# One block transformer decode step: 128 rows of the last gate's weights moved from the end of SP's queue to its beginning

## The chip, the core and the metric

One NeuronCore of a Trainium2 chip runs the whole program. The metric is the device time of one execution in microseconds (us); less is better. Three runs of the kernel before took 243.23, 243.19 and 242.94 us, median 243.19. PE is TensorE, DVE is VectorE, ACT is ScalarE, POOL is GpSimd, SP is SyncE, which here only issues DMAs. A DMA copies from the chip's memory (HBM) into SBUF, the cores' working memory of 128 partitions; sixteen DMA engines share the rows of each copy. PSUM holds the results of PE.

## What is computed

A decode step of one transformer block for four tokens (B = 4, D = 512). Six modulation vectors come from a condition `c`; attention over the last 2,048 entries of a cache, then a gated feed-forward part.

```python
mod = (_silu(c) @ w_mod).reshape(c.shape[0], 6, 1, -1)
sa, ca, ga, sb, cb, gb = (mod[:, 0], mod[:, 1], mod[:, 2], mod[:, 3], mod[:, 4], mod[:, 5])
h = _layernorm(x, axis=-1) * (1 + ca) + sa
x = x + ga * _A_ref(h, A_k_cache, A_v_cache, A_wq, A_wo)
h = _layernorm(x, axis=-1) * (1 + cb) + sb
x = x + gb * _B_ref(h, B_w1, B_w3, B_w2)
```

`_A_ref` is attention with 32 query heads over 8 key and value heads, head size 128, between the projections `wq` and `wo`. `_B_ref` is `(silu(x @ w1) * (x @ w3)) @ w2` with 1,792 hidden columns. All is float32. Some 101 MB are read once, most of it K and V. The last gate `gb` is `silu(c)` (4 x 512) times the last 512 columns of `w_mod` (512 x 512).

## The kernel before

Every weight and every piece of the cache comes by one long queue of DMAs that SP issues in a fixed, hand-written order (lines 91 to 125); ACT issues two more at the start, `t1_in` (the first query weights) and `x_in` (x, four rows). The order is: `t0_in` (c and the weights of sa and ca, into the first columns of the buffer KV1), the first K and V into KV0, the second K and V into KV1, then for each of four pairs of heads the weights WP and the next two K and V; at the end `wm_in` (weights of ga, sb, cb), `f1_in` and `f2_in` (w1 and w3), `gb_in` (the weights of gb) and six pieces of `w2_in`. Before an issue SP waits where its target is still in use: for `pe` 1 (KV1 still holds `t0_in`), `qt_done` (WP still holds query weights that are in use), `x_done` (a K and V has been used), `a_done`.

Each K and V is 128 rows of 64 KB, so KV0 and KV1 hold 8 MB each. The rows of a load are its partitions.

PE works through `main`, then four times through `pair` (scores, softmax turned on PE, values, output projection, for two heads) and `query` (the projection of the next queries), then `leave` and `post`. Other engines follow by semaphores that PE's instructions raise: `pe` counts the finished single steps. In `main` PE multiplies `sc`, the silu of c, by the weights of sa and ca into bank bM (8 products, line 255 by the helper `mm`), `pe` 1; then it transposes h (line 309), `pe` 2; then come the first queries.

The gate gb is made near the end: after `hid` has been put on its way, PE waits for `gb_in` (semaphore `dgb`), multiplies `sc` by its four blocks of 128 rows into four groups of partitions of bM, ACT copies the bank to `gb_sb` (line 458), and a product with `same` adds the four groups and turns the result (bT), which ACT copies to `gbJ`. Meanwhile PE takes w2 piece by piece as its six DMAs land. Behind the last piece DVE multiplies by gbJ (line 488), adds x1 (line 490), and SP stores the result (line 492).

```python
T.wait_ge(dgb, 16)
for k in range(4):
    ins = mm(bM[32 * k : 32 * k + B, :], sc[:, k * B : (k + 1) * B], KV[1][:, 6144 + 512 * k : 6144 + 512 * (k + 1)])
ins.then_inc(pe, 1)
A.wait((pe, 10))
t_gb = A.op(s.copy(gb_sb, bM))
```

Of the kernel before, what the change touches and what calls it, by code (L numbers as in the profile page):

```python
# [5 lines left out]
AF = mybir.ActivationFunctionType  # L6
# [4 lines left out]
B, D, HQ, G, SK, DH, W, FF = 4, 512, 32, 8, 8192, 128, 2048, 1792  # L11
P = 128
# [3 lines left out]
CHUNKS = [(j, c) for c in range(4) for j in range(4) if c < 2 or j < 3]  # L16
HEAD = 8
W2_CUTS = [0, 4, 8, 10, 12, 13, 14]
PAIRS = G // 2
# [23 lines left out]

def block_kernel(nc, x_in, t0_in, t1_in, kv_in, w_in, wm_in, f1_in, f2_in, gb_in, w2_in, out):
# [12 lines left out]
    A = Queue(nc, s, "act")  # L57
    V = Queue(nc, v, "dve")
    L = Queue(nc, gp, "pool")
    dx, dt0, dt1, dkv, dk, dva, dvb, dwo, dm, df1, df2a, df2b, dgb = sems("dx dt0 dt1 dkv dk dva dvb dwo dm df1 df2a df2b dgb")  # L60
    dw = sems(" ".join(f"dw{i}" for i in range(len(W2_CUTS) - 1)))
# [4 lines left out]
    KV = [sb("KV0", 16384), sb("KV1", 16384)]  # L66
    WP = sb("WP", 8192)
    T0 = KV[1][:, : 16 + 4096]
    x_sb = sb("x_sb", 512, B)
    ident, same, eps = sb("ident", P), sb("same", B), sb("eps", 1)  # L70
    sc, e1, e2 = sb("sc", 16), sb("e1", 16), sb("e2", 16)
    hT, h2T = sb("hT", 16), sb("h2T", 16)
    Z = sb("Z", B * 28)
    q_sb, p_sb, o_sb, a_sb, y_sb, g_sb, u_sb, gb_sb = [sb(n, 512) for n in "q_sb p_sb o_sb a_sb y_sb g_sb u_sb gb_sb".split()]
    pT = sb("pT", NT * B * 16)
# [12 lines left out]
    def load(dst, src, sem):  # L88
        S.dma_start(dst, src).then_inc(sem, 16)  # L89

    load(T0, t0_in, dt0)
    s.dma_start(WP[:, 4096:], t1_in).then_inc(dt1, 16)
    s.dma_start(x_sb, x_in).then_inc(dx, 16)
    load(KV[0], kv_in[0], dkv)
    S.wait_ge(pe, 1)
    load(KV[1], kv_in[1], dk)
    for p in range(PAIRS):
# [24 lines left out]
    load(KV[1][:, 3072:6144], f2_in[:, 3072:], df2b)  # L122
    load(KV[1][:, 6144:8192], gb_in, dgb)
    for a, b, sem in zip(W2_CUTS[:-1], W2_CUTS[1:], dw):
# [15 lines left out]
    for p in range(PAIRS - 1):  # L140
        gp.wait_ge(dk, 16 * (p + 1))
        for sem in (k_ok, va_ok, vb_ok):
            gp.sem_inc(sem, 1)
    for d, sem, n in ((dk, k_ok, 16 * PAIRS), (dva, va_ok, 16), (dvb, vb_ok, 16)):
        gp.wait_ge(d, n)
        gp.sem_inc(sem, 1)
# [24 lines left out]
    s.preload_act_table_set("natural_log_exp_and_others")  # L171
    for b_ in (bS, bQ, bO, bM):
        v_z = V.op(v.memset(b_, 0.0))
# [7 lines left out]
    A.wait((dt0, 16))  # L181
    t = A.op(s.activation(e1, T0[:, :16], AF.Exp, scale=-1.0))
    V.wait(t)
# [3 lines left out]
    V.wait(t, (dt0, 16))  # L187
    t_sc = V.op(v.tensor_mul(sc, T0[:, :16], e2))  # L188
# [7 lines left out]
    V.wait((pe, 2))  # L196
    t_hT = V.op(v.tensor_copy(hT, bT[:, :16]))  # L197
# [56 lines left out]
    def mm(o, lhsT, rhs, start=True, stop=True):  # L254
        return T.matmul(o, lhsT, rhs, start=start, stop=stop, skip_group_check=True)  # L255
# [47 lines left out]
    for k in range(4):  # L303
        for i in range(2):
            ins = mm(bM[32 * i : 32 * i + B, :], sc[:, k * B : (k + 1) * B], T0[:, 16 + (2 * k + i) * 512 : 16 + (2 * k + i + 1) * 512], k == 0, k == 3)
    ins.then_inc(pe, 1)
# [78 lines left out]
    ins.then_inc(pe, 1)  # L385
    A.wait((pe, 4))
    t_ga, t_sb, t_cb = [A.op(s.copy(dst, bX[32 * i : 32 * i + B, :])) for i, dst in enumerate((ga_sb, sb_sb, cb_sb))]

    V.wait((pe, 3), t_ga)
    t = V.op(v.tensor_mul(ag, bM[:B, :], ga_sb))  # L390
# [15 lines left out]
    ins.then_inc(pe, 1)  # L406
    V.wait((pe, 5))
    t_h2T = V.op(v.tensor_copy(h2T, bT[:, :16]))  # L408
# [11 lines left out]
    ins.then_inc(pe, 1)  # L420
    A.wait((pe, 6))
    t_g = A.op(s.copy(g_sb, bQ))
# [9 lines left out]
    ins.then_inc(pe, 1)  # L432
    A.wait((pe, 7))
    t = A.op(s.activation(view(eT), view(bP)[:, :, :, :B], AF.Exp, scale=-1.0))
# [7 lines left out]
    V.op(v.tensor_mul(view(hidT)[:, 0:2, 3], view(sT)[:, 0:2, 3], view(bP)[:, 2:4, 3, :B]))  # L442
    V.wait((pe, 8))
    t_u = V.op(v.tensor_copy(u_sb[:96], bA[:96]))
# [3 lines left out]
    ins.then_inc(pe, 1)  # L448
    V.wait((pe, 9))
# [12 lines left out]
    for i in range(len(W2_CUTS) - 1):  # L462
        T.wait_ge(dw[i], 16)
        for n in range(W2_CUTS[i], W2_CUTS[i + 1]):
            jj, c = CHUNKS[n]
            if n < HEAD:
                ins = mm(bO[32 * (n % 4) : 32 * (n % 4) + B, :], hw[:, c, jj, :], w2[:, n, :], n < 4, n >= HEAD - 4)
                continue
            for j in range(4):
                ins = mm(bX[32 * j : 32 * j + B, :P], hw[:, c, jj, :], w2[:, n, j * P : (j + 1) * P], n == HEAD, n == 13)  # L470
        if i == 0:
            T.wait_ge(A.sem, t_gb[1])
# [3 lines left out]
            A.wait((pe, 11))  # L476
            t_gb = A.op(s.copy(gbJ, bT[:, :P]))
        if i == 1:
            ins.then_inc(pe, 1)
            V.wait((pe, 12))  # L480
# [6 lines left out]
    V.wait((pe, 13), t_gb)  # L487
    t = V.op(v.tensor_mul(yt, bX[:, :P], gbJ))  # L488
# [8 lines left out]
def _layout(i):  # L497
    import numpy as np

    def a(t):  # L500
        return np.ascontiguousarray(t)

    k = i["A_k_cache"][:, :, SK - W :, :].reshape(B, G, NT, 512, DH)
    v = i["A_v_cache"][:, :, SK - W :, :].reshape(B, G, NT, 4, P, DH)
    k = k.transpose(1, 4, 2, 0, 3).reshape(G, P, 8192)
    v = v.transpose(1, 4, 2, 0, 3, 5).reshape(G, P, 8192)
    wm = i["w_mod"].reshape(4, P, 6, 512).transpose(1, 0, 2, 3)
    c = i["c"].reshape(B, 4, P).transpose(2, 1, 0).reshape(P, 16)
    wq = i["A_wq"].reshape(4, P, G, 512).transpose(2, 1, 0, 3).reshape(G, P, 2048)
# [5 lines left out]
    return {  # L515
        "x_in": a(i["A_x"].reshape(B, D)),
        "t0_in": np.concatenate([c, wm[:, :, 1::-1].reshape(P, 4096)], 1),
        "t1_in": np.concatenate([wq[0], wq[1]], 1),
        "kv_in": np.concatenate([k, v], 2),
        "w_in": np.stack([np.concatenate(p, 1) for p in pairs]),  # L520
        "wm_in": a(wm[:, :, 2:5]).reshape(P, 6144),
        "f1_in": np.concatenate([w1, w3[:, :, 1536:]], 2).reshape(P, 8192),
        "f2_in": a(w3[:, :, :1536]).reshape(P, 6144),
        "gb_in": a(wm[:, :, 5]).reshape(P, 2048),
        "w2_in": a(np.stack([w2[4 * j + c_] for j, c_ in CHUNKS], 1)).reshape(P, 14 * D),
    }
# [15 lines left out]
```

## Time and profile before

| what | value |
|---|---|
| median of three runs | 243.19 us (242.94 to 243.23) |
| the profiled execution's own time | 243.12 us |
| its span in the trace | 241.8 us |
| PE busy | 136.2 us (56%) |
| DVE busy | 38.6 us (16%) |
| ACT busy | 25.1 us (10%) |
| mean granted TensorE clock | 0.852 |

The span runs from the first to the last instruction on the core; the profiled execution's own time is 1.32 us longer. A busy share is a mean over the whole span. The mean share of the DMA engines counts all sixteen alike: a share of 0.19 can be three engines that work all the time while thirteen rest. In the page's part on queues, q1 is SP's, q10 ACT's, and "instruction" the loading of the program itself. A "chain" is followed back from the last instruction, at each step to what released it.

### The profile page before, as it was taken

Reading aid. Unit: us, or ns where it says so; the run is one execution under the profiler, and the core shown is the slowest. Engines: PE = TensorE matmul, PEld = TensorE weight load, DVE = VectorE, ACT = ScalarE, POOL = GpSimd, SP = SyncE. Lnnn points to the kernel's source line nnn. Section 1 sums busy time; section 2 is a strip of 40 time slices with the busy share of each in tenths; the row PEclk is TensorE's granted clock in tenths of the full one; section 3 lists DMA queues with packets and bytes.
Section 4 is the critical chain, followed back from the end, with each engine's and each line's share of the span. In section 5 each row is a group of like instructions: output and inputs, shape, how many; then the busy total and the mean of one; then the engine's idle time right before and its main releaser. Section 6 shows DMA issues by size and latency. Waiting matters only on the chain. (4 is left out here: it accounts for less than half of the span.)

```text
span 241.8 us, 2271 instructions
## 1 busy us (share of the span) xinstructions
PE 136.2 (56%) x940; PEld 37.3 (15%) x940; DVE 38.6 (16%) x126; ACT 25.1 (10%) x54; POOL 1.7 (1%) x14
## 2 busy tenths in 40 slices
PE   3004677817660387276723772667237768665964
PEld 0000121201210012112200121112001222111211
DVE  3003202202200022022000220220002222124122
ACT  2002002100120002001100020001001201123110
POOL 2000000000000000000000000000000000000000
PEclk9999959967996579987985798879858997995999
DMA  7998989899989898999898989998989999999992
GB/s 266 451 500 369 499 371 488 379 417 445 493 379 488 369 499 381 407 428 510 369 499 369 499 369 423 434 510 369 499 350 442 442 400 440 453 431 396 418 411 106
DMA packets 4044, 101.33 MB, mean 419 GB/s; under 512 B 452, under 2 KB 580, under 8 KB 1096
## 3 DMA queue, kind: packets, MB, share of 16 engines
q1 hardware_dynamic: 3888, 99.17, 95.6%
q10 hardware_dynamic: 152, 2.11, 2.1%
q8 instruction: 3, 0.05, 0.1%
q14 instruction: 1, 0.01, 0.0%
HBM read 101.20 MB, written 0.07 MB: 419 GB/s over the span
## 5 line engine op out<-in xcount | busy, mean ns | idle before, releaser
L255 PE MATMUL bS<-KV,Z 128*16 128x512 f32 x256 | 42.5, 824 | 38.8 <-PEq L258 38.8
L255 PE MATMUL bO<-KV,pT 128*16 128x512 f32 x256 | 31.9, 642 | 0.5
L255 PEld LDWEIGHTS bS<-KV,Z 128*16 128x16 f32 x256 | 9.1, 122 | 66.6 <-issue 66.6
L218 DVE TENSOR_REDUCE MX<-bS 128x1 f32<-128x512 f32 x8 | 5.5, 691 | 79.6 <-PE bS L255 79.6
L255 PE MATMUL bM<-KV,sc 128*4 128x512 f32 x24 | 7.3, 835 | 16.6 <-DVE sc L188 16.6
L367 ACT ACTIVATE p_sb<-bS,NB 128x512 f32<-128x512 f32 x8 | 5.5, 687 | 101.2 <-ACTq L358 101.2
L276 PE MATMUL bP<-ident,p_sb 128*128 128x128 f32 x32 | 5.0, 280 | 17.3 <-PEq L258 17.3
L255 PE MATMUL bA<-WP,oT 128*4 128x512 f32 x64 | 10.4, 728 | 5.2 <-PEq L258 5.2
L255 PEld LDWEIGHTS bO<-KV,pT 128*16 128x16 f32 x256 | 8.1, 105 | 22.9 <-issue 22.9
L372 ACT ACTIVATE o_sb<-bO,LB 128x512 f32<-128x512 f32 x8 | 5.5, 687 | 48.7 <-ACTq L358 48.7
L255 PE MATMUL bQ<-WP,hT 128*4 128x512 f32 x64 | 9.2, 648 | 0.6 <-DVE hT L197 0.6
L276 PE MATMUL bX<-ident,o_sb 128*128 128x128 f32 x32 | 5.0, 280 | 7.9 <-PEq L258 7.9
L244 DVE TENSOR_REDUCE oT<-bX 128x16 f32<-128x64 f32 x8 | 1.8, 224 | 44.0 <-PE bX L276 44.0
L276 PE MATMUL bT<-ident,q_sb 128*128 128x128 f32 x32 | 5.5, 298 | 3.6 <-PEq L258 3.6
L276 PEld LDWEIGHTS bP<-ident,p_sb 128*128 128x128 f32 x32 | 3.4, 140 | 24.4 <-issue 24.4
L276 PEld LDWEIGHTS bX<-ident,o_sb 128*128 128x128 f32 x32 | 3.4, 141 | 15.0 <-issue 15.0
L227 DVE COPY pT<-bP 128x256 f32<-128x256 f32 x8 | 3.4, 424 | 13.7 <-PE bP L276 13.7
L255 PE MATMUL bQ<-KV,h2T 128*4 128x512 f32 x32 | 5.3, 831 | 0.3 <-DVE h2T L408 0.3
L276 PEld LDWEIGHTS bT<-ident,q_sb 128*128 128x128 f32 x32 | 3.7, 150 | 8.3 <-issue 8.0
L255 PEld LDWEIGHTS bM<-KV,sc 128*4 128x4 f32 x24 | 1.0, 106 | 22.6 <-DVE sc L188 18.2
L255 PE MATMUL bX<-KV,sc 128*4 128x512 f32 x24 | 4.4, 592 | 0.0
L202 DVE TENSOR_REDUCE Z<-bT 128x16 f32<-128x64 f32 x8 | 1.8, 224 | 15.4 <-PE bT L276 15.1
(101 smaller groups left out, 68.0 us busy)
## 6 DMA issues: line engine op xcount, KB each, us to landing
WP<-w_in SPq DMA_DIRECT2D x3, 4096.0 KB, 18.9
KV<-kv_in SPq DMA_DIRECT2D x1, 4096.0 KB, 24.1
KV<-f_in SPq DMA_DIRECT2D x1, 4096.0 KB, 25.9
KV<-kv_in SPq DMA_DIRECT2D x1, 3072.0 KB, 30.9
KV<-wm_in SPq DMA_DIRECT2D x1, 3072.0 KB, 16.5
KV<-f_in SPq DMA_DIRECT2D x2, 1536.0 KB, 17.2
KV<-t_in SPq DMA_DIRECT2D x1, 2056.0 KB, 12.3
WP<-t_in ACTq DMA_DIRECT2D x1, 2048.0 KB, 12.5
```

The source lines that it names most:

```text
L202: v.tensor_reduce(Z.rearrange("p (b i) -> p b i", b=B)[:, :, 12 : 12 + R], bT.rearrange("p (r k i) -> p i r k", r=R, k=4)[:, :B], axis=AX. ...
L218: t = V.op(v.reduce_max(MX[:, 0:1], bS, axis=AX.X))
L227: v.tensor_copy(pT.rearrange("p (t b c r) -> p c b t r", t=NT, b=B, c=4), bP.rearrange("p (c b i) -> p c b i", c=4, b=B)[:, :, :, :16].rea ...
L244: V.op(v.tensor_reduce(oT.rearrange("p (r b) -> p r b", r=R), diag, axis=AX.X, op=ALU.add), ot_ok)
L255: return T.matmul(o, lhsT, rhs, start=start, stop=stop, skip_group_check=True)
L276: ins = T.transpose(dst[:, c * P : (c + 1) * P], src[:, c * P : (c + 1) * P], ident)
L367: A.op(s.activation(p_sb, bS, AF.Exp, bias=NB[:, 0:1], accum_out=SM[:, 0:1]), p_ok)
L372: A.op(s.mul(o_sb, bO, LB[:, 0:1]), o_ok)
```

## The change

Of the 512 rows of weights of gb, the last 128 leave `gb_in`, which so has 1,536 columns instead of 2,048. They come in `gc_in`, an array of 12 rows with 5,632 columns: 132 rows of weights (the last four zero) as eleven blocks of twelve. The matching columns of c, eleven blocks of four columns in the first twelve partitions, come as 44 more columns of `t0_in`; the silu is taken of these, too.

SP issues `gc_in` right behind `t0_in`, ahead of the first K and V, into columns 8192 to 13823 of KV1 on partitions 0 to 11. PE multiplies the eleven blocks behind sa and ca, into bank bX, and ACT copies the bank to a new tile, `g3_sb`. The bank is set to zero by DVE before. KV1's second half is in use by `gc_in` until `pe` 2, so the second K and V is loaded in two halves: the first waits for `pe` 1 as before, the other for `pe` 2. All later counts of `pe`, and POOL's counts of `dk`, are one higher. At the end PE makes three products in place of four, and DVE adds `g3_sb` to the bank (the fourth group of partitions of bM is not written there and is zero) in place of ACT's copy.

```diff
+SUB, ROWS = 11, 12
+C_IN = 16 + 4 * SUB
-    T0 = KV[1][:, : 16 + 4096]
+    T0 = KV[1][:, : C_IN + 4096]
+    GC = KV[1][:ROWS, 8192 : 8192 + SUB * 512]
...
     s.dma_start(x_sb, x_in).then_inc(dx, 16)
+    load(GC, gc_in, dgc)
     load(KV[0], kv_in[0], dkv)
     S.wait_ge(pe, 1)
-    load(KV[1], kv_in[1], dk)
+    load(KV[1][:, :8192], kv_in[1][:, :8192], dk)
+    S.wait_ge(pe, 2)
+    load(KV[1][:, 8192:], kv_in[1][:, 8192:], dk)
...
-    load(KV[1][:, 6144:8192], gb_in, dgb)
+    load(KV[1][:, 6144:7680], gb_in, dgb)
...
-    for b_ in (bS, bQ, bO, bM):
+    for b_ in (bS, bQ, bO, bM, bX):
...
+    A.wait((pe, 2))
+    t_g3 = A.op(s.copy(g3_sb, bX))
...
     ins.then_inc(pe, 1)
+    T.wait_ge(dgc, 16)
+    for m in range(SUB):
+        j = m % 4
+        ins = mm(bX[32 * j : 32 * j + B, :], sc[:ROWS, 16 + m * B : 16 + (m + 1) * B], GC[:, 512 * m : 512 * (m + 1)], m < 4, m >= SUB - 4)
+    ins.then_inc(pe, 1)
     T.wait_ge(V.sem, t_h[1])
...
     T.wait_ge(V.sem, t_hT[1])
+    T.wait_ge(A.sem, t_g3[1])
     T.wait_ge(dt1, 16)
...
-    for k in range(4):
+    for k in range(3):
         ins = mm(bM[32 * k : 32 * k + B, :], sc[:, k * B : (k + 1) * B], KV[1][:, 6144 + 512 * k : 6144 + 512 * (k + 1)])
     ins.then_inc(pe, 1)
-    A.wait((pe, 10))
-    t_gb = A.op(s.copy(gb_sb, bM))
+    V.wait((pe, 11), t_g3)
+    t_gb = V.op(v.tensor_add(gb_sb, bM, g3_sb))
```

On SP, at the program's beginning, the queue before was as follows (a row is a load's target, its source and its shape in partitions and columns):

```order
L89 DMA KV<-t_in 128x4112
L89 DMA KV<-kv_in 128x16384 x2
L89 DMA WP<-w_in 128x8192
L89 DMA KV<-kv_in 128x16384 x2
L89 DMA WP<-w_in 128x8192
```

and in the changed kernel it is:

```order
L92 DMA KV<-t_in 128x4156
L92 DMA KV<-gc_in 12x5632
L92 DMA KV<-kv_in 128x16384
L92 DMA KV<-kv_in 128x8192 x2
L92 DMA WP<-w_in 128x8192
L92 DMA KV<-kv_in 128x16384 x2
```

One load of twelve rows has come in ahead of the first K and V, and the second K and V has become two loads.

On PE, in `main` and at the head of `pair`, there stood before (bM takes the products for sa and ca, bT the transposes of h, bS the first scores):

```order
L255 MATMUL bA<-y_sb 128x512
L255 MATMUL bM<-KV,sc 4x512 x8
L309 MATMUL bT<-ident,h 128x4 x4
L313 UNCONDITIONAL_BRANCH
L318 REGISTER_ALU
L255 MATMUL bS<-KV,Z 16x512 x16
```

and now:

```order
L263 MATMUL bA<-y_sb 128x512
L263 MATMUL bM<-KV,sc 4x512 x8
L263 MATMUL bX<-KV,sc 4x512 x11
L322 MATMUL bT<-ident,h 128x4 x4
L327 UNCONDITIONAL_BRANCH
L332 REGISTER_ALU
L263 MATMUL bS<-KV,Z 16x512 x16
```

Eleven products into bX now stand ahead of the transposes of h, and so ahead of all of pair 0. Of the four products of gb at the end of PE's program three are left, at the same place.

More of the change, by code (lines that the diff above doesn't have):

```diff
@@ L41, in op, with block_kernel @@
         return (self.sem, self.n)
-def block_kernel(nc, x_in, t0_in, t1_in, kv_in, w_in, wm_in, f1_in, f2_in, gb_in, w2_in, out):
+def block_kernel(nc, x_in, t0_in, t1_in, kv_in, w_in, wm_in, f1_in, f2_in, gb_in, gc_in, w2_in, out):
     T, v, s, gp, S = nc.tensor, nc.vector, nc.scalar, nc.gpsimd, nc.sync
@@ L59, in block_kernel @@
     L = Queue(nc, gp, "pool")
-    dx, dt0, dt1, dkv, dk, dva, dvb, dwo, dm, df1, df2a, df2b, dgb = sems("dx dt0 dt1 dkv dk dva dvb dwo dm df1 df2a df2b dgb")
+    dx, dt0, dt1, dkv, dk, dva, dvb, dwo, dm, df1, df2a, df2b, dgb, dgc = sems("dx dt0 dt1 dkv dk dva dvb dwo dm df1 df2a df2b dgb dgc")
     dw = sems(" ".join(f"dw{i}" for i in range(len(W2_CUTS) - 1)))
@@ L67, in block_kernel @@
     WP = sb("WP", 8192)
-    T0 = KV[1][:, : 16 + 4096]
+    T0 = KV[1][:, : C_IN + 4096]
+    GC = KV[1][:ROWS, 8192 : 8192 + SUB * 512]
     x_sb = sb("x_sb", 512, B)
     ident, same, eps = sb("ident", P), sb("same", B), sb("eps", 1)
-    sc, e1, e2 = sb("sc", 16), sb("e1", 16), sb("e2", 16)
+    sc, e1, e2 = sb("sc", C_IN), sb("e1", C_IN), sb("e2", C_IN)
     hT, h2T = sb("hT", 16), sb("h2T", 16)
     Z = sb("Z", B * 28)
-    q_sb, p_sb, o_sb, a_sb, y_sb, g_sb, u_sb, gb_sb = [sb(n, 512) for n in "q_sb p_sb o_sb a_sb y_sb g_sb u_sb gb_sb".split()]
+    q_sb, p_sb, o_sb, a_sb, y_sb, g_sb, u_sb, gb_sb, g3_sb = [sb(n, 512) for n in "q_sb p_sb o_sb a_sb y_sb g_sb u_sb gb_sb g3_sb".split()]
     pT = sb("pT", NT * B * 16)
@@ L140, in block_kernel @@
     for p in range(PAIRS - 1):
-        gp.wait_ge(dk, 16 * (p + 1))
+        gp.wait_ge(dk, 16 * (p + 2))
         for sem in (k_ok, va_ok, vb_ok):
             gp.sem_inc(sem, 1)
-    for d, sem, n in ((dk, k_ok, 16 * PAIRS), (dva, va_ok, 16), (dvb, vb_ok, 16)):
+    for d, sem, n in ((dk, k_ok, 16 * (PAIRS + 1)), (dva, va_ok, 16), (dvb, vb_ok, 16)):
         gp.wait_ge(d, n)
@@ L181, in block_kernel @@
     A.wait((dt0, 16))
-    t = A.op(s.activation(e1, T0[:, :16], AF.Exp, scale=-1.0))
+    t = A.op(s.activation(e1, T0[:, :C_IN], AF.Exp, scale=-1.0))
     V.wait(t)
@@ L187, in block_kernel @@
     V.wait(t, (dt0, 16))
-    t_sc = V.op(v.tensor_mul(sc, T0[:, :16], e2))
+    t_sc = V.op(v.tensor_mul(sc, T0[:, :C_IN], e2))
     A.wait((pe, 1))
     t_sa = A.op(s.copy(sa_sb, bM[32 : 32 + B, :]))
+    A.wait((pe, 2))
+    t_g3 = A.op(s.copy(g3_sb, bX))
     V.wait((pe, 1), t_r)
@@ L195, in block_kernel @@
     t_h = V.op(v.scalar_tensor_tensor(h, xs, st1[:, 7:8], sa_sb, op0=ALU.mult, op1=ALU.add))
-    V.wait((pe, 2))
+    V.wait((pe, 3))
     t_hT = V.op(v.tensor_copy(hT, bT[:, :16]))
@@ L304, in block_kernel @@
         for i in range(2):
[L305 removed]
+            ins = mm(bM[32 * i : 32 * i + B, :], sc[:, k * B : (k + 1) * B], T0[:, C_IN + (2 * k + i) * 512 : C_IN + (2 * k + i + 1) * 512], k == 0, k == 3)
+    ins.then_inc(pe, 1)
[3 more added lines that the diff above has]
+        ins = mm(bX[32 * j : 32 * j + B, :], sc[:ROWS, 16 + m * B : 16 + (m + 1) * B], GC[:, 512 * m : 512 * (m + 1)], m < 4, m >= SUB - 4)
     ins.then_inc(pe, 1)
@@ L385, in block_kernel @@
     ins.then_inc(pe, 1)
-    A.wait((pe, 4))
+    A.wait((pe, 5))
     t_ga, t_sb, t_cb = [A.op(s.copy(dst, bX[32 * i : 32 * i + B, :])) for i, dst in enumerate((ga_sb, sb_sb, cb_sb))]
-    V.wait((pe, 3), t_ga)
+    V.wait((pe, 4), t_ga)
     t = V.op(v.tensor_mul(ag, bM[:B, :], ga_sb))
@@ L406, in block_kernel @@
     ins.then_inc(pe, 1)
-    V.wait((pe, 5))
+    V.wait((pe, 6))
     t_h2T = V.op(v.tensor_copy(h2T, bT[:, :16]))
@@ L420, in block_kernel @@
     ins.then_inc(pe, 1)
-    A.wait((pe, 6))
+    A.wait((pe, 7))
     t_g = A.op(s.copy(g_sb, bQ))
@@ L432, in block_kernel @@
     ins.then_inc(pe, 1)
-    A.wait((pe, 7))
+    A.wait((pe, 8))
     t = A.op(s.activation(view(eT), view(bP)[:, :, :, :B], AF.Exp, scale=-1.0))
@@ L442, in block_kernel @@
     V.op(v.tensor_mul(view(hidT)[:, 0:2, 3], view(sT)[:, 0:2, 3], view(bP)[:, 2:4, 3, :B]))
-    V.wait((pe, 8))
+    V.wait((pe, 9))
     t_u = V.op(v.tensor_copy(u_sb[:96], bA[:96]))
@@ L448, in block_kernel @@
     ins.then_inc(pe, 1)
-    V.wait((pe, 9))
+    V.wait((pe, 10))
     t_hid = V.op(v.tensor_mul(view(hidT)[:, :, :3], view(sT)[:, :, :3], view(bS)[:, :, :3, :B]))
     T.wait_ge(dgb, 16)
-    for k in range(4):
+    for k in range(3):
         ins = mm(bM[32 * k : 32 * k + B, :], sc[:, k * B : (k + 1) * B], KV[1][:, 6144 + 512 * k : 6144 + 512 * (k + 1)])
     ins.then_inc(pe, 1)
-    A.wait((pe, 10))
-    t_gb = A.op(s.copy(gb_sb, bM))
+    V.wait((pe, 11), t_g3)
+    t_gb = V.op(v.tensor_add(gb_sb, bM, g3_sb))
     T.wait_ge(V.sem, t_hid[1])
@@ L471, in block_kernel @@
         if i == 0:
-            T.wait_ge(A.sem, t_gb[1])
+            T.wait_ge(V.sem, t_gb[1])
             for j in range(4):
@@ L475, in block_kernel @@
             ins.then_inc(pe, 1)
-            A.wait((pe, 11))
+            A.wait((pe, 12))
             t_gb = A.op(s.copy(gbJ, bT[:, :P]))
@@ L479, in block_kernel @@
             ins.then_inc(pe, 1)
-            V.wait((pe, 12))
+            V.wait((pe, 13))
             t_y = V.op(v.tensor_copy(y_sb, bO))
@@ L486, in block_kernel @@
     ins.then_inc(pe, 1)
-    V.wait((pe, 13), t_gb)
+    V.wait((pe, 14), t_gb)
     t = V.op(v.tensor_mul(yt, bX[:, :P], gbJ))
@@ L508, in _layout @@
     c = i["c"].reshape(B, 4, P).transpose(2, 1, 0).reshape(P, 16)
+    cs = np.zeros((P, SUB * B), c.dtype)
+    last = np.zeros((SUB * ROWS, B + 512), c.dtype)
+    last[:P, :B] = i["c"].reshape(B, 512)[:, 384:].T
+    last[:P, B:] = i["w_mod"][384:, 5 * 512 :]
+    last = last.reshape(SUB, ROWS, B + 512).transpose(1, 0, 2)
+    cs[:ROWS] = last[:, :, :B].reshape(ROWS, SUB * B)
     wq = i["A_wq"].reshape(4, P, G, 512).transpose(2, 1, 0, 3).reshape(G, P, 2048)
@@ L516, in _layout @@
         "x_in": a(i["A_x"].reshape(B, D)),
-        "t0_in": np.concatenate([c, wm[:, :, 1::-1].reshape(P, 4096)], 1),
+        "t0_in": np.concatenate([c, cs, wm[:, :, 1::-1].reshape(P, 4096)], 1),
         "t1_in": np.concatenate([wq[0], wq[1]], 1),
@@ L523, in _layout @@
         "f2_in": a(w3[:, :, :1536]).reshape(P, 6144),
-        "gb_in": a(wm[:, :, 5]).reshape(P, 2048),
+        "gb_in": a(wm[:, :3, 5]).reshape(P, 1536),
+        "gc_in": a(last[:, :, B:]).reshape(ROWS, SUB * 512),
         "w2_in": a(np.stack([w2[4 * j + c_] for j, c_ in CHUNKS], 1)).reshape(P, 14 * D),
```

## The prediction

> **What bounds the kernel now.** I read the page first, for the queues and the chain that ended last, then that chain in order of time, then narrow windows over the last microseconds.
>
> ```profile
> span 241.8 us, 2271 instructions
> DMA packets 4044, 101.33 MB, mean 419 GB/s; under 512 B 452, under 2 KB 580, under 8 KB 1096
> q1 hardware_dynamic: 3888, 99.17, 95.6%
> q10 hardware_dynamic: 152, 2.11, 2.1%
> q8 instruction: 3, 0.05, 0.1%
> q14 instruction: 1, 0.01, 0.0%
> DMA 11%; SPq 1%; PE 0%; DVE 0%; issue 0%
> ```
>
> The queues' shares add up to 97.8% of sixteen engines over the whole span: the mean DMA engine is never idle but at the two ends. One engine's pace while it works is therefore 419 / (16 x 0.978) = 26.8 GB/s, or 0.61 us for 16 KB. Beside SP's (q1) and ACT's loads (q10), four blocks of instructions pass through the same engines.
>
> ```profile
> 212.29 26.78 DMA KV<-w_in
> 239.06 0.04 issue
> 239.11 0.45 PE bX L255 x8
> 239.57 0.30 DVE yt L488
> 239.90 0.29 DVE y L490
> ```
>
> In the chain in order of time the last piece of w2, issued at 212.29, lands 26.78 us later, at 239.06. Behind it stand 0.45 of PE, two operations of DVE and the store. The change leaves that tail of 2.7 us alone, so the end moves by as much as the landing at 239.06 moves. How do the engines stand there?
>
> ```profile
> 236.50:237.00 0.50, 0.38 (x16) 0.32 (x16) 0.50 (x1) 0.00 (x0) 0.00 (x0) 1.00 0.93 328
> ...
> 237.30:237.70 0.40, 0.00 (x0) 1.00 0.20 77
> 237.70:238.00 0.30, 0.00 (x0) 1.00 0.18 68
> 238.00:238.30 0.30, 0.00 (x0) 1.00 0.12 48
> 238.30:238.60 0.30, 0.00 (x0) 1.00 0.14 55
> 238.60:239.00 0.40, 0.00 (x0) 1.00 0.00 0
> ```
>
> In these windows the last two columns are the mean busy share of the sixteen DMA engines and GB/s (the first row shows all engines of the core, the others DVE alone). Until 237 all are busy (0.93). From 237.3 a share of 0.20 to 0.18 means three engines out of sixteen (0.19 x 16 = 3.0), from 238.0 it means two (0.13 x 16 = 2.1), and from 238.6 none. Thirteen engines are done by about 237.3, two work until 238.6. So **the kernel ends with its two latest DMA engines, 1.3 us behind the crowd**, and a third stands about 0.65 us behind it. The mean load is not the bound.
>
> Why they are late, no view says in so many words, but sizes fit. Three windows that hold one instruction block each, 94 to 96, 213 to 216 and 236.9 to 241 us, give:
>
> ```profile
> q14 instruction: 1, 0.01, 1.0%
> ...
> q8 instruction: 1, 0.02, 2.3%
> ...
> q8 instruction: 1, 0.02, 1.7%
> ```
>
> A block holds its engine for 2.3% of 16 x 3 us = 1.1 us (the last: 1.7% of 16 x 4.1 = 1.1). Every load before spreads 128 rows evenly, so an engine that carried a block stays behind to the end. The last block came when the crowd had finished.
>
> **The change part by part.** Durations are of this one execution: span 241.8, whole time 243.12 us, 0.07 below the median of three, 243.19.
>
> *Taken off the end.* gb_in loses a fourth of each row: 8 rows x 2 KB = 16 KB on each of sixteen engines, 0.61 us at 26.8 GB/s. Two rows check this on the late engines themselves, for there a piece of w2 is also 128 rows of 2 KB:
>
> ```profile
> 238.49 0.11 PEld L255 LDWEIGHTS bX<-KV,hidT 128*4 128x4 f32 x8 [0.29 <-DMA KV<-w_in]
> 239.10 0.11 PEld L255 LDWEIGHTS bX<-KV,hidT 128*4 128x4 f32 x8 [0.51 <-DMA KV<-w_in]
> ```
>
> PE was let go by the last two pieces 239.10 - 238.49 = 0.61 us apart. So **-0.61** for every engine.
>
> *Added for every engine.* c grows by 44 columns: 8 rows x 176 B = 1,408 B, **+0.05**. The second K and V is split, 64 KB rows into two of 32 KB. Windows 64 to 78 us (64 KB rows alone) and 102.5 to 108.5 (32 KB rows alone):
>
> ```profile
> q1 hardware_dynamic: 96, 6.29, 103.7%
> ...
> q1 hardware_dynamic: 80, 2.62, 101.6%
> ```
>
> One 64 KB row takes 1.037 x 14 x 16 / 96 = 2.420 us, two of 32 KB 2 x 1.016 x 6 x 16 / 80 = 2.438. Eight rows an engine: at most 8 x 0.018 = 0.15, at least 0 (the bytes are the same); I take the middle, **+0.07**.
>
> *Added for some.* The twelve rows of gc_in are 22,528 B each. No load of the trace before has twelve rows. One row an engine would be 0.84 us on twelve engines and nothing on four (0.84 = 22,528 B / 26.8 GB/s). Spread evenly over sixteen it would be 0.63 on each. I take the first, since one unbroken row is the piece in which every load here moves.
>
> So a left-out engine gains 0.61 - 0.05 - 0.07 = **0.49 us**, and one of the twelve loses 0.84 - 0.49 = **0.35 us**. The crowd, landing some 1.3 us before the latest, can take +0.35 unseen; what decides is on which side the two latest engines stand.
>
> [...]
>
> *The start.* The eleven products stand on PE between bM and the transposes of h. Everything in pair 0 that needs q moves with them, and with it SP's first WP load, which waits for qt_done.
>
> ```profile
> 17.85 0.67 DVE L175 TENSOR_REDUCE st<-x_sb 4x1 f32<-4x512 f32 x1 [14.82 <-DMA x_sb<-x_in]
> 21.25 6.27 PE L255 MATMUL bM<-KV,sc 128*4 128x512 f32 x16 [16.65 <-DVE sc L188]
> 42.97 0.33 SPq L89 DMA_DIRECT2D WP<-w_in  x1
> 211.27 4.01 PE L255 MATMUL bX<-KV,sc 128*4 128x512 f32 x22
> WP<-w_in SPq DMA_DIRECT2D x3, 4096.0 KB, 18.9
> ```
>
> Eleven products took 4.01 us at 211.27 (22 records are eleven matmuls) and would take 11 x 6.27 / 8 = 8.6 at the start's pace. As PE has by then worked for six microseconds I expect 4 to 7. The cover is SP's queue: WP, issued at 42.97, landed a median 18.9 us later, of which its 4 MB need 10.0 at 419 GB/s; 8.9 us it stood behind the second K and V. So up to 8.9 us of delay the engines do not run dry. Part of it also comes back. x, for which DVE waits to 17.85, has its small rows behind the first 64 KB row of K and V (2.4 us) and its completion behind the next; now gc_in's rows of 0.84 us stand there, so x may land 0 to 4 us earlier, and sc, bM and the rest with it. Cost: nothing. The split's second half waits for the eleven products, but its first half (4 MB, 10 us of transfer behind the first K and V) covers that. SP's extra issues go out while the first load runs.
>
> *The end of PE, ACT and DVE.* One matmul less, and the copy of gb becomes an addition on DVE behind hid. Both are ready microseconds before w2's second piece, for which PE waits; nothing. One DVE memset lies in the wait for x. ACT's copy of the early products stands ahead of the first q copy, under the same cover of 8.9 us.
>
> *Instruction blocks.* Eleven matmuls more ahead and one less behind move the later part of PE's program ten matmuls on, and the block that came at 236.9 comes ten matmuls earlier, inside the stream: its engine, now among the crowd, would get +1.1 and end at 237.3 + 1.1 = 238.4, less 0.49 if left out, or plus 0.35.
>
> **Rivals.** The **forecast**: the two latest engines and the third are left out. They end at 238.6 - 0.49 = 238.1, the crowd at 237.3 + 0.35 = 237.65, under them. Time: 243.12 - 0.49 = 242.63, and on the median's scale 243.19 - 0.49 = **242.70**.
>
> **First rival, on the other side:** one of the two latest engines is among the twelve. Then the 0.84 us stand on the path, and the time is 243.19 + 0.35 = 243.54, slower. It decides as soon as a single one of the two is there. For it speaks that twelve is three quarters of sixteen; against it, that the engines of the instruction blocks look like a fixed few: following packets by their end times in the trace, the first block's engine is none of the four that carried x_in's four rows. [...]
>
> **Second:** only part is gained, since the third engine, or that of the block that moves, is among the twelve. The third ends at 238.0 + 0.35 = 238.35, 0.25 below 238.6; the moved block's at 238.4 + 0.35 = 238.75, slightly above: 242.9 to 243.35.
>
> **Third:** the eleven products run at the slow pace and x comes no earlier. Then 8.6 us use up the 8.9, and with an issue's latency (the 64 KB store needed 1.5 us in all) the engines idle up to 1.2 us: 243.9 to 244.7, depending on the first rival. It decides from about 7.4 us of delay.
>
> **Fourth:** gc_in spreads over all sixteen. Then each engine has -0.49 + 0.63 = +0.14: 243.33.
>
> **How the numbers follow.** Forecast 0.50, first rival 0.25, second 0.13, third 0.06, fourth 0.06. The forecast stands right at the bound of 0.2% (0.49 us of 243.19), about the least that a measurement of this kernel can tell from no change, so half of its chance counts as faster and half as the same; the first rival's +0.14% is mostly the same. Faster: 0.25 and a little of the second, 0.27. Slower: the third and a fifth of the first, 0.11. Same: 0.62. The range leaves out the third rival and little else: from 242.70 less 0.25 (a split that costs nothing and the spread of the three times) to the first rival's 243.54 and 0.1 of spread: 242.45 to 243.65.
>
> **What would show it.** In narrow windows at the end of the changed kernel, a DMA share that falls from full later and stays at two or three engines for about half a microsecond rather than 1.3 bears the forecast out; a gap that stays or grows to 1.6 us, the first rival. The chain must still end in w2's last piece. WP's first issue at 44 to 51 with DMA shares near 1 from 40 to 62 us shows that the start is covered; a window below 0.9 there is the third rival. The block of 236.9 should show at 232 to 235. I am wrong altogether if the chain ends in PE or DVE, or in another load.

## The result, and the profile after

| kernel | median (range, runs) | ratio to before, 95% interval |
|---|---|---|
| before | 243.10 us (242.94 to 243.23, 4) | 1 |
| changed | 245.87 us (245.32 to 246.38, 4) | 1.0114 (1.0090 to 1.0137) |

The change costs 2.77 us where a gain of 0.49 was forecast. The profiled execution of the changed kernel took 245.32 us, the fastest of its four, 2.20 more than the 243.12 of before; its span is 243.9 us, 2.1 more. From the page of the changed kernel, the span, the DMA totals and SP's queue:

```profile
span 243.9 us, 2315 instructions
DMA packets 4212, 101.36 MB, mean 416 GB/s; under 512 B 480, under 2 KB 608, under 8 KB 1252
q1 hardware_dynamic: 4056, 99.20, 95.9%
```

The bytes are the same to 0.03 MB, and the engines' share on q1 has not fallen (95.6% before). The engines are therefore not idle for longer; they work for 2 us longer on the same bytes. The last steps of the chain that ended last in the changed kernel, in order of time (start, length, step):

```profile
217.59 23.58 DMA KV<-w_in
241.17 0.04 issue
241.21 0.45 PE bX L263 x8
241.68 0.30 DVE yt L502
242.01 0.29 DVE y L504
```

The chain is the one of before. The last piece of w2 lands at 241.17 instead of 239.06, 2.11 us later, and this is the whole growth of the span. So the question is where the engines lost these 2.11 us and the 0.49 that they were to gain.

They lost them at the start. The traffic of the six microseconds from 12 to 18 us, when `gc_in` and the first rows of K and V move, first before, then changed (one line of the DMA view each; a packet is what one engine moves in one piece, here a row, or four bytes behind an engine's last row):

```profile
DMA packets 84, 3.09 MB, mean 515 GB/s; under 512 B 33, under 2 KB 33, under 8 KB 37
```

```profile
DMA packets 92, 2.11 MB, mean 352 GB/s; under 512 B 48, under 2 KB 48, under 8 KB 52
```

0.98 MB are missing, but this shows only where to look. A packet counts whole in the window where it begins, and rows of 64 KB begin in sets of sixteen, 2.42 us apart, so the edges of the window alone can move such a sum by up to 1 MB. How much was lost stands in the packets themselves, in the kept trace. In the changed kernel twelve packets of 22,528 B begin between 12.06 and 12.43 us: one row on each of twelve engines, as the prediction had it. But they take 1.71 to 2.79 us, not 0.84. And the first row of K and V on each engine, 2.42 us before, is slow on all sixteen: 4.89 to 4.91 us on the four engines that have no row of `gc_in`, 2.94 to 3.80 us on the other twelve. One line of the DMA view shows these twelve, which begin from 13.3 to 15.5 us together with twelve four-byte packets:

```profile
q1 hardware_dynamic: 24, 0.79, 121.2%
```

That is 1.212 x 16 x 2.2 / 12 = 3.56 us a row. From the second rows on it is 2.42 us again. So the four engines without a row lost 4.90 - 2.42 = 2.5 us. The twelve ended their first row of K and V at 17.85 to 18.17 us, where without `gc_in` it would have ended at 14.5 to 14.85: they lost 3.3 us.

The first K and V shows the loss when it lands. SP's issue and the time from issue to landing (the last number), before:

```profile
1.16 0.43 SPq L89 DMA_DIRECT2D KV<-kv_in  x1
...
KV<-kv_in SPq DMA_DIRECT2D x1, 31.2
```

and changed:

```profile
1.66 27.31 SPq L92 DMA_DIRECT2D KV<-kv_in  x3
...
KV<-kv_in SPq DMA_DIRECT2D x1, 34.7
```

It lands at 36.4 instead of 32.4, 4.0 us later, where one row of `gc_in` on an engine was to cost 0.84. Not all of the 4.0 us is the load's: fifteen engines have landed their part by 35.60, and the sixteenth, at 36.39, carried an instruction block from 34.26 to 35.36 us. In run e10 (below), which has the same load, issued at 1.65, and no block at that time, the same row of the view is

```profile
KV<-kv_in SPq DMA_DIRECT2D x1, 33.9
```

so the load's part is 35.6 - 32.4 = 3.2 us.

A second thing went wrong at the start, on PE. The timeline of PE in the changed kernel from the eleven products on (start, busy; in brackets the idle time before and what ended it):

```profile
25.84 2.75 PE L263 MATMUL bX<-KV,sc 12*4 12x512 f32 x22
28.52 0.41 PE L322 MATMUL bT<-ident,h 4*128 4x4 f32 x4
36.79 1.89 PE L263 MATMUL bQ<-WP,hT 128*4 128x512 f32 x8 [7.86 <-issue]
```

The eleven products took 2.75 us, and the transposes of h stand at 28.52, 0.56 earlier than before (29.08), since x came earlier. But the first queries, which stood at 30.10 with 0.61 us of waiting for hT, now stand at 36.79 after 7.86 us of "issue", the name for a wait that no semaphore explains. SP's first WP goes with them:

```profile
50.34 0.33 SPq L92 DMA_DIRECT2D WP<-w_in  x1
```

That is 7.4 us later than the 42.97 of before. So there were two suspects, a load that holds the engines up and a WP that comes too late, and the runs had to tell them apart.

### The profile page after: what moved, and what is told of

Its sections match the earlier page's. It is cut to its first block, busy times and chain, and to the rows that moved or that the text cites. A ratio compares the mean times of both kernels' runs of the same rounds, so it can differ in the third digit from the quotient of the medians.

```text
span 243.9 us, 2315 instructions
## 1 busy us (share of the span) xinstructions
PE 136.2 (56%) x960; PEld 38.0 (16%) x960; DVE 40.2 (16%) x128; ACT 25.2 (10%) x54; POOL 1.7 (1%) x14
## 3 DMA queue, kind: packets, MB, share of 16 engines
q10 hardware_dynamic: 152, 2.11, 2.1%
## 5 line engine op out<-in xcount | busy, mean ns | idle before, releaser
L263 PE MATMUL bS<-KV,Z 128*16 128x512 f32 x256 | 41.0, 798 | 35.7 <-PEq L266 35.7
L263 PE MATMUL bO<-KV,pT 128*16 128x512 f32 x256 | 30.1, 611 | 0.5
L284 PE MATMUL bP<-ident,p_sb 128*128 128x128 f32 x32 | 6.4, 335 | 17.2 <-PEq L266 17.2
L263 PE MATMUL bM<-KV,sc 128*4 128x512 f32 x22 | 6.7, 802 | 15.6 <-DVE sc L194 15.6
L263 PE MATMUL bA<-WP,oT 128*4 128x512 f32 x64 | 10.9, 759 | 4.1 <-PEq L266 4.0
L284 PEld LDWEIGHTS bP<-ident,p_sb 128*128 128x128 f32 x32 | 4.2, 169 | 24.4 <-issue 24.4
L263 PE MATMUL bX<-KV,sc 128*4 128x512 f32 (+1 forms) x46 | 6.4, 590 | 0.7 <-DMA KV<-wm_in 0.7
L379 ACT ACTIVATE q_sb<-bQ 128x512 f32<-128x512 f32 x4 | 2.4, 597 | 19.3 <-ACTq L372 19.3
```

The source lines that it names most:

```text
L284: ins = T.transpose(dst[:, c * P : (c + 1) * P], src[:, c * P : (c + 1) * P], ident)
L379: A.op(s.mul(q_sb, bQ, DH**-0.5), q_ok)
```

## The experiments

The **landing theory** (P in the expectations) says that the twelve rows are slow because they land in twelve neighbouring partitions, and that what they hold up holds up the other engines' K and V too. Its rivals: the **source theory** (S), by which the twelve rows of `gc_in`, neighbours in HBM as well, are slow to read; theory R, by which any load on fewer than sixteen engines holds up the rest; and theory M, by which the load is harmless and PE's delay makes the loss. Times of before beside these runs were 243.05 to 243.08 us.

| run | what differs from the changed kernel | median (range, runs) | ratio to before (95%) |
|---|---|---|---|
| e1 | twelve rows, every ninth partition | 244.49 (243.93 to 245.29, 4) | 1.0050 (1.0033 to 1.0067) |
| e2 | twelve rows, every second partition | 244.65 (244.39 to 245.89, 5) | 1.0062 (1.0045 to 1.0079) |
| e3 | source rows some 150 KB apart | 245.73 (245.63 to 246.37, 4) | 1.0118 (1.0101 to 1.0135) |
| e4 | 128 rows of 2 KB, one product | 243.26 (243.04 to 243.44, 10) | 1.0007 (0.9998 to 1.0017) |
| e5 | eight rows of 32 KB, every fourth partition | 243.81 (243.29 to 244.18, 6) | 1.0033 (1.0021 to 1.0046) |
| e6 | the same eight rows in partitions 0 to 7 | 246.80 (246.68 to 248.18, 4) | 1.0172 (1.0145 to 1.0199) |
| e7 | one product instead of eleven | 245.83 (245.43 to 245.99, 4) | 1.0118 (1.0102 to 1.0133) |
| e8 | no `gc_in`, products of zeros | 245.11 (243.53 to 245.40, 5) | 1.0075 (1.0049 to 1.0101) |
| e9 | as e8, `query` ahead of `pair` in PE's program | 242.63 (242.36 to 242.99, 11) | 0.9980 (0.9971 to 0.9989) |
| e10 | the change, `query` ahead of `pair` | 245.79 (245.29 to 246.03, 4) | 1.0113 (1.0098 to 1.0129) |
| e11 | as e5, `query` ahead of `pair` | 243.33 (242.99 to 243.90, 11) | 1.0015 (1.0005 to 1.0025) |

### Where the rows land, and where they come from

**e1 and e2** keep the twelve rows and their bytes and put them farther apart (STEP is 9 in e1, 2 in e2). The partitions between them are set to zero first, and SP waits for that, so that it issues `gc_in` at 9.5 us instead of 1.17.

```diff
-    GC = KV[1][:ROWS, 8192 : 8192 + SUB * 512]
+    GCZ = KV[1][:REACH, 8192 : 8192 + SUB * 512]
+    GC = KV[1][0:REACH:STEP, 8192 : 8192 + SUB * 512]
+    S.wait_ge(V.sem, 6)
+    V.op(v.memset(GCZ, 0.0))
```

> The twelve rows of gc_in go to partitions 0, 9, 18 ... 99 in place of 0 to 11; DVE sets the region between them to zero first, and c's columns stand in the same partitions. Source, number of rows and their length are as in the change. [...] Theory S (the source: 270 KB read from one small piece of memory) and theory R (any load on fewer than sixteen engines stalls the rest): nothing changes, 245.3 to 246.4. Theory M (the late start of pair 0 on PE, where the first queries start at 36.78 in place of 30.10, costs the time): nothing changes, 245.3 to 246.4.

> As e1, but with the rows in every second partition, 0, 2 ... 22, which by theory P is twice the spread of the change and half that of e1: the load's stay falls to about half of the change's 3.2 us and the time to about 244.2 (243.8 to 244.7). Theories S, R and M: 245.3 to 246.4.

Measured: 244.49 and 244.65 us. Both gain over the changed kernel, by 1.4 and 1.2 us; e2 is where the landing theory had put it, e1 is not: the theory gave it 242.6 to 243.4 us, for the wide spread should have given back nearly all. (Twice the change's spread is e2's step of 2; that this is half of e1's, whose step is 9, was the author's estimate, and no run shows it.) The traffic of 12 to 18 us in e1:

```profile
DMA packets 97, 2.34 MB, mean 391 GB/s; under 512 B 48, under 2 KB 48, under 8 KB 52
```

This lies between the change (2.11 MB) and before (3.09), but so near to the change that the window's edges could make the difference. The packets say more: in e1 the twelve rows take 0.84 to 1.58 us, but the first rows of K and V still take 2.60 to 4.04 us; in e2 they take 0.95 to 1.58 and 2.84 to 4.19 us. So the place matters, but it isn't enough that the twelve rows are far from each other. Some of what is left may come from the test itself: with `gc_in` issued late, the engines stand idle for 0.2 us on average between 12 and 20 us in both runs, 0.01 us in the change. PE's wait is there, too (7.07 and 7.74 us), but WP goes out at 45.74 and 46.58 us and the engines are not idle then. The miss gave the theory a sharper form, an estimate of the author that no view shows: a row is slow where it lands in the way of another engine, which is carrying K and V at that time.

**e3** leaves the landing place as the change has it and takes the source rows apart in HBM.

```diff
-    load(GC, gc_in, dgc)
+    load(GC, gc_in[:, : SUB * 512], dgc)
...
-        "gc_in": a(last[:, :, B:]).reshape(ROWS, SUB * 512),
+        "gc_in": np.concatenate([a(last[:, :, B:]).reshape(ROWS, SUB * 512), np.zeros((ROWS, 32768), c.dtype)], 1),
```

> The change with gc_in's twelve rows 150 KB apart in memory (each row is followed by columns that no one reads); the landing place is that of the change. Theory S: the rows take 0.84 us and the time falls to 242.6 to 243.4. Theories P, R and M: as the change, 245.3 to 246.4.

Measured: 245.73 us, as slow as the change, with 1.72 MB from 12 to 18 us and rows that take 1.56 to 2.94 us. The source theory falls.

**e4** spreads the same weights over all 128 partitions as every other load does (SUB, ROWS = 1, 128), and one product takes them.

> The early load as 128 rows of 2 KB over all 128 partitions, with one product in place of eleven; place in the queue, split K and V and the end of the kernel are as in the change. Theories P, S and R: no stall and no engine is spared, so the sum is the split's 0.05 to 0.15 us and what a few more small rows cost: 243.1 to 243.4. Theory M: with one product the first queries start about where they stood before, so 243.1 to 243.4, too; it is told apart by e1 and by the runs without products.

Measured: 243.26 us, no change against before, and 3.25 MB from 12 to 18 us: the engines aren't held up. But nothing is gained either; 16 KB an engine have only been moved from the end to the start.

**e5 and e6** are the sharp test: sixteen blocks of eight rows, 32 KB a row, the same bytes and products in both, and the region between set to zero in the same way. SP waits for that, and `gc_in` is issued at 7.90 us in both. Only the step between the partitions differs, 4 in e5 and 1 in e6, and with it how many partitions are set to zero. That at a step of 4 no row is in another engine's way was the author's estimate, and what is forecast for e5 by the sharper form rests on it.

```diff
-SUB, ROWS = 11, 12
+SUB, ROWS, STEP = 16, 8, 4
...
+    L.op(gp.memset(GCZ[:, 4096:], 0.0))
+    V.op(v.memset(GCZ[:, :4096], 0.0))
```

> The same 128 weight rows as sixteen blocks of eight, with 32 KB each, in partitions 0, 4 ... 28 (DVE and POOL set the region between to zero). [...] The rows then take 1.2 us, the windows from 12 to 18 us carry some 3.1 MB, eight engines end later by 1.22 - 0.46 = 0.76 us and the others earlier by 0.46. If the two latest engines of the kernel before are among those others the time is 242.6; if the third, 0.65 us before them, is among the eight, up to 243.2. Theory R (any load on few engines stalls the rest): 245 or more. [...]

> As e5, but in partitions 0 to 7, two groups of four neighbours. [...] Theory R: as e5, whatever that gives.

Measured: 243.81 and 246.80 us, 2.99 apart. e6 is where the landing theory had put it, at 246.5 to 248; e5 is above the 242.6 to 243.2 of the theory's sharper form, but below the 245 or more of theory R. From 12 to 18 us there moved in e5, and then in e6:

```profile
DMA packets 97, 2.91 MB, mean 485 GB/s; under 512 B 44, under 2 KB 44, under 8 KB 48
```

```profile
DMA packets 71, 1.42 MB, mean 236 GB/s; under 512 B 42, under 2 KB 42, under 8 KB 46
```

In e5 the packets show no loss at all: the eight rows take 1.21 us each, a pace of 27 GB/s, and every row of K and V takes its 2.42 us. In e6 the eight rows take 2.77 to 4.07 us, and the first rows of K and V 5.80 us on the eight engines without a row. So a load on few engines is not slow in itself, and theory R falls with e5.

At the same time x arrives, whose four small rows queue behind `gc_in`. DVE's first operation on it in e5, then in e6:

```profile
14.48 0.67 DVE L187 TENSOR_REDUCE st<-x_sb 4x1 f32<-4x512 f32 x1 [6.61 <-DMA x_sb<-x_in]
```

```profile
18.18 0.67 DVE L187 TENSOR_REDUCE st<-x_sb 4x1 f32<-4x512 f32 x1 [10.31 <-DMA x_sb<-x_in]
```

Eight rows side by side hold up x, behind them, by 3.7 us more than eight rows four partitions apart. That the landing place decides is shown by this pair; by what path inside the memory is not something these views show. The sizes go with it: the change's twelve rows, 270,336 bytes in partitions 0 to 11, are under way from 12.06 to 15.23 us, 3.2 us; e6's eight, 262,144 bytes in partitions 0 to 7, are under way for 4.5 us, and e6 is the slowest of all. Distance alone doesn't give e1, whose twelve rows lie nine partitions apart and whose first rows of K and V still take 2.60 to 4.04 us. The sharper form fits these numbers and e5's undisturbed rows, but it was not shown: no view tells which engine writes to which partition, and e5 has eight rows, and e1 twelve.

### The products, and a wait without a semaphore

**e7** keeps the load and makes one of the eleven products; **e8** keeps the eleven products, made with zeros, and leaves out the load. Both leave out a part of gb, as e9 does below.

```diff
-    for m in range(SUB):
+    for m in range(1):
```

```diff
-    load(GC, gc_in, dgc)
...
-    T.wait_ge(dgc, 16)
...
-        ins = mm(bX[32 * j : 32 * j + B, :], sc[:ROWS, 16 + m * B : 16 + (m + 1) * B], GC[:, 512 * m : 512 * (m + 1)], m < 4, m >= SUB - 4)
+        ins = mm(bX[32 * j : 32 * j + B, :], sc[:ROWS, 16 + m * B : 16 + (m + 1) * B], zero[:ROWS, :], m < 4, m >= SUB - 4)
```

> The change with one of the eleven early products left in and ten left out (the output lacks their part); the load and all waits stay. Theories P and R: the load alone costs the time, 245.2 to 246.4. Theory M (the late pair 0 on PE): with ten products gone the first queries start at about 29 to 31, and the time is 242.7 to 243.5.

> The change without the load of gc_in: the eleven products are made with a tile of zeros (the output lacks the part of the last 128 rows). Theories P and R: every engine has 16 KB less to carry at the end and nothing more at the start, 243.06 - 0.49 = 242.57, whatever PE does in pair 0. Theory M: pair 0 starts as late as in the change, 245.2 to 246.4.

Measured: e7 245.83 us, the time of the change, though its first queries come at 28.08 after 0.61 us of waiting and its WP is issued at 45.97, not 50.34. So the load by itself costs what the change costs, and theory M falls as the cause of the change's loss. But e8, without the load, takes 245.11 us, where 242.6 was to be expected if only the load did harm. In e8 the six microseconds carry 3.15 MB; nothing is held up there. PE and SP show another loss:

```profile
36.70 1.89 PE L262 MATMUL bQ<-WP,hT 128*4 128x512 f32 x8 [6.96 <-issue]
```

```profile
50.45 0.33 SPq L92 DMA_DIRECT2D WP<-w_in  x1
```

and the windows around WP's issue have gaps (busy time of DVE, granted clock, mean share of the sixteen engines, GB/s):

```profile
48.00:50.00 2.00, 0.25 (x3) 1.00 1.10 475
50.00:51.00 1.00, 0.90 (x4) 1.00 0.25 98
51.00:52.00 1.00, 0.57 (x3) 1.00 1.73 492
52.00:53.00 1.00, 0.00 (x0) 1.00 0.17 66
```

As a packet counts whole where it begins, a share can be above 1, and a low one alone is no idle time. Before, whose engines never stop there, the windows have this line, too:

```profile
49.00:50.00 1.00, 0.00 (x0) 1.00 0.00 0
```

The packets show what is idle. In e8 fourteen engines end their last rows of the second K and V at 50.81 to 51.29 us and begin their first rows of WP at 51.41 to 52.34. A fifteenth, as far as its packets can be followed, ends at 52.45 and begins at 54.22. That is 0.6 us of idle time for the mean engine; before, the change and e9 have none there. The fifteen first rows then take 1.46 to 2.34 us, where 32 KB take 1.21 elsewhere. So few rows begin from 52 to 53 us because most are under way, and the low share there is no second stop.

What does PE wait for? Its queries are in the body `query`, to which `main` jumps and which stands behind the long body `pair` in the program. The eleven products put 44 more instructions of PE ahead of it (22 records each of products and weight loads). **Theory F**, an estimate that no view shows: PE holds only the next stretch of its program; the jump now leaves that stretch, and the block with `query` has to be loaded. In e8 a block of instructions is under way from 34.25 to 35.29 us. The DMA view from 34 to 36 us, in e8:

```profile
q8 instruction: 1, 0.02, 3.2%
```

The first queries start 1.4 us after its end. That distance, 1.41 to 1.43 us, stands in all seven runs with the long wait (the change, e1, e2, e3, e5, e6 and e8, 6.91 to 7.86 us). In the other six PE waits for hT alone, and no block ends shortly ahead of the queries. Before has a block in this window, too, but its queries had begun at 30.10; the block by itself is no sign of a wait. What PE waits for in the five microseconds until the block begins isn't in a view; that the block stands in line behind rows of K and V is likely, and not shown.

**e9** tests it. It is e8 with `query` written ahead of `pair`; no instruction is added or taken away.

```diff
+    with nc.body("query", parent=root, valid_engines=[ET.PE]):
+        project(0)
+        take(q_ok)
+        turn(bT, q_sb, qt_done)
+        nc.br("pair", engines=[ET.PE])
```

(The same five lines go from behind `pair`.)

> e8 (no load of gc_in, eleven products of zeros; the output lacks the last 128 rows' part) with the block of instructions 'query' placed ahead of 'pair' in PE's program; the order of execution is the same. In e8 PE stood still for 6.96 us before the first queries, with an instruction block on its way through a DMA engine from 34.25, SP issued WP at 50.45 in place of 42.97, and around 51 to 51.5 the queue ran dry. Theory F (the eleven products push 'query' past the end of the instructions that PE holds; the fetch makes WP late): with the block near, the first queries start at 31 to 33, WP is issued at 43 to 46, the queue does not run dry, and the time falls by 2 us or more to 242.4 to 242.8. Theory K (the late start comes from the eleven products themselves or from the waits for them): nothing changes, 244.7 to 245.4.

Measured: 242.63 us, 2.5 less than e8, and the wait is gone:

```profile
31.52 1.89 PE L262 MATMUL bQ<-WP,hT 128*4 128x512 f32 x8 [0.48 <-DVE hT L204]
```

WP is issued at 45.23. In this kernel the jump's distance costs 2.5 us (245.11 against 242.63). How much of its program PE holds was not shown: what the runs show is that the wait of 6.96 us is there with `query` behind `pair` and gone with it ahead. The idle time and the slow rows of WP explain about 1.3 of the 2.5 us, as a mean over the engines. The rest stands on one engine: in e8's profiled execution it lands its part of the last piece at 240.69 us, the next one at 239.13. It is likely the one whose first row of WP began only at 54.22; no view names the engines.

### The two together

**e10** is the change with `query` moved in the same way; **e11** is e5 with it.

> The changed kernel with 'query' ahead of 'pair', nothing else. The twelve rows' stall is still there. Theories P and F together: the two losses cover the same hole, since the stall makes the second K and V late by 3 us and with it the time at which WP is needed; so mending PE alone gives next to nothing, 245.2 to 246.2. If the losses simply added up, it would fall by the 2.5 us that e8 lost against 242.6: 243 to 243.6.

> [...] Theories P and F: e5 still had PE idle for 7.20 us before the first queries, WP issued at 48.99 and some engines waiting for it at 51; that goes, 0.8 to 1.2 us off e5's 243.81: 242.5 to 243.0, under the kernel before. If only P holds, as e5, 243.6 to 244.

Measured: e10 245.79 us, though its first queries stand at 29.23 and its WP goes out at 45.63. In the change the second K and V is itself some 3 us late, so a late WP finds the queue still full, and taking PE's wait away gives nothing. The two losses do not add up: 2.5 us of the one lie within the other.

e11 against e5 gives the same wait of PE (7.20 us) another price, 0.48 us instead of 2.5, and the ranges of the two overlap. In e5 x came early and WP went out at 48.99, 1.5 us ahead of e8's; its engines are idle for 0.03 us around 51 us, e8's for 0.6. So the price hangs on when WP goes out; from which time on a wait costs was not measured.

e11, with neither loss, took 243.33 us, 0.25 above the 243.08 of before, and above the 242.5 to 243.0 that it was given. PE is in order there:

```profile
28.17 1.49 PE L269 MATMUL bQ<-WP,hT 128*4 128x512 f32 x8 [0.66 <-DVE hT L211]
```

Its eleven times lie in two groups, near 243.05 and near 243.8. The end of its profiled execution (243.13 us) in windows with the same columns as above:

```profile
236.50:237.00 0.50, 0.35 (x1) 1.00 0.91 328
237.00:237.50 0.50, 0.34 (x1) 1.00 0.66 254
237.50:238.00 0.50, 0.00 (x0) 1.00 0.28 107
238.00:238.50 0.50, 0.00 (x0) 1.00 0.09 33
```

The end still is a few late engines. Six land their part of the last piece by 237.52 us, eight from 237.96 to 238.38, about 1 us later, as eight engines with 32 KB more would, and the last two at 238.64 and 238.95. One that carries an instruction block and is also among those eight would explain the miss; this is the prediction's second rival in another kernel, and it was argued, not tested.

## Why the prediction was wrong, point by point

- **What bounds the kernel: right.** The chain ends in the last piece of w2, PE and DVE behind it take what they took, and the span grew by what the landing moved.
- **Taken off the end, -0.61 + 0.05 + 0.07: right.** e9 has these terms without `gc_in`'s row: 242.63 against 243.08 us beside it, -0.45 (95%: -0.27 to -0.70), where -0.49 was worked out for an engine without a row.
- **`gc_in`, 0.84 us on twelve engines and nothing on four: the step that failed.** The price was the duration of one unbroken row at 26.8 GB/s, the pace of an engine in the 128-row loads. The rows took 1.71 to 2.79 us, and what a row takes depends on where it lands (32 KB: 1.21 us in e5, 2.77 to 4.07 in e6); the engines without a row were held up with them. The two latest engines were given 0 for it. Their landing moved by +2.11 with -0.49 in it, so the term was 2.6 us for them; the packets at the start give 2.5 us for an engine without a row, and 3.3 us instead of 0.84 for one of the twelve. On the profiled executions the sum closes: 243.12 - 0.49 + 2.5 = 245.1 us (245.32). That no load before had twelve rows was said in the prediction, and the bounds were taken from 0.63 to 0.84 all the same; both ends assumed the same pace.
- **Which engines are late: it fits the forecast's side, but isn't shown.** The gap between the crowd and the latest was to shrink from 1.3 to about half a microsecond, or grow to 1.6 by the first rival. The end of the changed kernel, in the same windows:

```profile
239.00:239.50 0.50, 0.20 (x1) 1.00 0.89 340
239.50:240.00 0.50, 0.00 (x0) 1.00 0.58 205
240.00:240.30 0.30, 0.00 (x0) 1.00 0.26 82
240.30:240.70 0.40, 0.00 (x0) 1.00 0.19 72
240.70:241.00 0.30, 0.00 (x0) 1.00 0.00 0
```

  From 240.0 a share of 0.26 means four engines, and all have stopped by 240.7. By its landings the last piece has a gap of 0.75 us, from 240.42 to 241.17 (1.34 before, from 237.72 to 239.06). But the gap did not shrink by the term that the forecast had. Against e9, which lacks the load, the crowd lands 3.2 us later and the latest engine 2.5 us, close to the 3.3 us that an engine with a row and the 2.5 us that one without lost at the start. So the latest are likely among the four without a row, which was the forecast's choice. That choice, a term of 0 for the two latest, no run shows: the packets show twelve engines with one row each and four with none, and no view names the engines; at 2.5 us lost by the four and 3.3 by the twelve it no longer decided anything.
- **The start, "Cost: nothing": wrong, though it did not show.** The products' delay was overrated, 2.75 us where 4 to 7 were expected, and the cover, too: before, the rows of the first WP begin at 50.67 us, 7.7 and not 8.9 us after its issue, and in e8 it takes 1.0 us from the issue to the first row. As allowed, x came earlier by 1.4 us (DVE on it at 16.46, before 17.85). What was not counted is the distance of PE's jump: 7.86 us of waiting where the sum had none. Of the steps listed, "instruction blocks" asked only what a block does to its DMA engine, not who waits for it.
- **The third rival** had the right place and the right point: WP was issued 7.4 us later, about the 7.4 from which it was to decide. Its cause was another (the long wait behind the jump, not slow products), and its price larger: e8 against e9 gives 2.5 us where 1.2 was worked out. In the change itself it was covered by the other loss (e10). The sign named for it, a window under 0.9, can't be read in windows of a microsecond, as the 0.00 from 49 to 50 us before shows.
- **The moved block:** one was expected to go from 236.9 to 232 or 235. The last one still comes behind 236.9 in the change. The one that stood between 213 and 216 us in before is not there, and one has come in at 40.13 us. The block that ends at 35.36 us, 1.43 ahead of the first queries, is the one at 34.26.
- **The fourth rival** (`gc_in` over all sixteen, 243.33) did not happen, but e4 does by hand what it describes and took 243.26.

## What to carry to other kernels

Price a DMA by the partitions in which it lands, not only by its bytes and the engines that share it: the same bytes at the head of a full queue made a kernel 3 us slower when eight rows lay side by side than when they lay four partitions apart (e6 246.80, e5 243.81), and what stood behind them paid for it. When instructions are put ahead of a jump, look for a wait behind it that no semaphore names, and try the program with the body that is used next ahead of the long one: here the wait fell from 6.96 to 0.48 us and the time by 2.5 (e8, e9). And when two losses fall into the same stretch, mending one alone may show nothing (e7 245.83, e10 245.79, the change 245.87), so undo both before either is cleared.

## What the runs showed of the hardware that was not expected

- A load of 0.26 MB held up more than itself: engines without a row of it took 4.9 us for their next 64 KB in the change and 5.8 us in e6, where they took 2.42 us in e5 and before.
- With eleven or sixteen products ahead of a jump PE stood still for 6.91 to 7.86 us (e6 6.91, e8 6.96, e5 7.20, the change 7.86), until 1.41 to 1.43 us after the end of a block of instructions of 16 KB, 1.0 to 1.1 us of one DMA engine; with `query` ahead of `pair` the wait was gone (e9 0.48, e10 0.64, e11 0.66). No semaphore names it: the profile shows "issue".
- Engines that had run dry in e8 were slow at first: the first rows of WP took 1.46 to 2.34 us on the fifteen engines that had stood idle, where 32 KB take 1.21 us elsewhere in that run. Why was not looked into.
